# A planned single-core kernel: copies of y and of the outputs out of PSUM move from ScalarE to VectorE from token block 7 on, with a new order of all steps

## The chip, the cores and the metric

The kernel runs on one core of a Trainium2 chip. A core has five engines that run side by side, each with its own queue, in order: TensorE (matmuls; PE in the profile, its weight loads PEld), VectorE (DVE), ScalarE (ACT), GpSimd (POOL) and SyncE (SP, which here only issues DMAs). Matmul results land in PSUM, which GpSimd does not touch in this kernel; everything else is in SBUF. Engines wait for each other by semaphores. The metric is device time in microseconds of one launch; before the change the median of 13 runs is 299.23 us (295.42 to 300.69).

## What is computed

The reference is a gated linear recurrence followed by a gated feed-forward layer:

```python
q, k, v, a_re, a_im                     # (4, 8, 768, 48), fp32
mag = sqrt(a_re**2 + a_im**2)
scale = minimum(mag, 0.999) / (mag + 1e-6)
for t in range(768):                    # a = (a_re + i a_im) * scale
    S_re, S_im = ar*S_re - ai*S_im + k_t v_t^T, ar*S_im + ai*S_re
    y[:, :, t] = q_t @ S_re
x = y laid out as (3072 tokens, 384)
out = (sigmoid(x @ w_gate) * (x @ w_val)) @ w_out      # 384 -> 1536 -> 384
```

Inputs and output are fp32; the kernel's matmul operands are fp16 apart from the two prefix sums.

## The kernel before

The 3072 tokens are cut into 24 blocks of 128 (4 batches of 6 blocks), and these into ten groups of 1, 2, 2, 2, 3, 3, 3, 3, 3, 2 blocks (SIZES). A block m is (batch b, place c in the batch).

The recurrence is done in chunks. For each group ScalarE squares a (L597), GpSimd adds and clips (L614, L622), ScalarE takes logarithms and a reciprocal by exp (L629, L635, L640), GpSimd multiplies the ratio (L650) and ScalarE takes its arctangent (L714). For each block TensorE forms prefix sums of the log magnitude (`cl`, L656) and of the phase (`ct`, L734); ScalarE makes the decays e^(+-x/2) (`ee`, L662, L664), which GpSimd multiplies into q and k (L708); VectorE rounds the phase to whole turns (`r16`, L762), TensorE subtracts the turns (`nid`, L769), ScalarE makes sine and cosine (`cs`, L786 to L789), and VectorE multiplies them into k and q (`ks`, `qs`, L797). The k and q of a block are transposed by TensorE and copied by VectorE (`tp`, `qkT`, L838, L847) up to block 12, and by DMA (`xk`, `xq`, L820) from block 13 on (CROSS = 13). TensorE forms scores (`sc`, L859), VectorE masks them (`mst`, L868), and TensorE forms y (`y`, L933, L935) and the state update (`kv`, L904). VectorE carries the state (`u`, `P`, L885, L914) and GpSimd casts it to fp16 (`x16`, L895).

The phase runs on from block to block. In batch 0 GpSimd adds up a running sum (`run`, L750) which TensorE sums in (L737). In the other batches ScalarE copies the last row of a block's phase (`cr`, L777), a DMA from GpSimd's queue adds it to the first row of the next block's (`hop`, L726), and that block's `ct` waits for it.

Then y is copied out of PSUM and scaled to fp16 (`y16`), transposed (`xp`, L952) and copied (`xt`, L958). For a group the layer is done in 12 slices of 128 of the inner width: two matmuls of three steps each (`pg`, `pv`, L972), tanh on ScalarE (L982; the sigmoid is (tanh(x/2)+1)/2), the product on VectorE (`p`, L988), and the output matmul (`po`, L1007) for each block, in three parts. The output is copied out of PSUM with a factor 0.5 (`ot`) and stored from SP (`st`, L1025). ScalarE's functions lie in three table sets, loaded in turn (L1035). PSUM holds four buffers for the layer (`moe`) and four for the rest (`gen`).

Both copies out of PSUM go through one helper; the engine is chosen by the block's number:

```python
def scaled(m, dst, src, f):
    if m >= EASE:
        nc.vector.tensor_scalar(out=dst, in0=src, scalar1=f, scalar2=1.0,
                                op0=ALU.mult, op1=ALU.mult)
    else:
        nc.scalar.activation(out=dst, in_=src, func=FT.Copy, scale=f)
```

On ScalarE it is L517 in the profile, on VectorE L514. With EASE = 13, 13 blocks are on each side of y (13 and 11) and of the output (13, and 11 blocks with 12 copies, since the last block's output goes in two halves).

No loop nest sets the order. Every step is entered into a plan under a key such as ("y16", 7), with the steps it must follow, and the table TIMES holds one number for each step. The steps are sorted by that number and issued so, which fixes the order in each engine's queue. A second table, WARM, holds runs of matmuls on a zero tile (L1042) that are sorted in between, and the table loads stand in TIMES as well. The numbers are sort keys: no instruction waits for a time.

Of the kernel before, what the change touches and what calls it, by code (L numbers as in the profile page):

```python
# [27 lines left out]
EASE = 13  # L28
# [9 lines left out]
        12.8, 25.15, 38.52],  # L38
    "wo": [
        43.82, 55.48, 63.41],  # L40
# [3 lines left out]
        4.3, 7.5, 16.28, 25.26, 34.34, 41.35, 49.21, 65.37, 71.79,  # L44
        77.54, 86.69, 96.07, 100.42, 113.48, 117.83, 124.09, 136.17,
        143.42, 150.02, 165.27, 171.53, 176.33, 193.74, 203.66],
# [3 lines left out]
        7.5, 22.16, 40.13, 54.96, 83.64, 106.1, 133.38, 157.24, 181.89,  # L50
        208.31],
    "add": [
        8.05, 23.66, 26.43, 42.11, 45.62, 62.44, 66.74, 86.01, 87.1,
        88.59, 108.24, 110.3, 112.3, 135.68, 136.76, 138.25, 159.57,
        163.06, 164.66, 184.03, 191.35, 192.43, 212.12, 214.58],
    "min": [
        8.65, 25.92, 27.52, 45.1, 47.16, 65.26, 68.58, 88.08, 89.56,
        90.07, 113.78, 111.78, 114.29, 137.74, 139.23, 139.74, 161.99,
        164.15, 165.74, 185.12, 194.27, 194.79, 213.2, 218.63],
    "lna": [  # L60
        9.44, 29.36, 44.52, 66.4, 89.75, 117.39, 140.72, 169.31, 197.35,
        226.36],
    "lnm": [
        9.06, 28.66, 47.78, 69.2, 90.76, 118.4, 141.74, 170.32, 196.34,
        225.29],
    "inv": [
        9.99, 30.22, 45.39, 69.9, 91.78, 119.8, 142.75, 171.34, 198.54,
        227.23],
    "r": [
        10.53, 31.22, 32.2, 47.67, 49.15, 73.67, 72.7, 93.39, 95.85,  # L70
        94.36, 121.16, 123.11, 122.14, 145.09, 147.04, 146.06, 175.94,
        172.97, 173.95, 200.7, 199.73, 201.68, 229.64, 228.16],
    "cl": [
        9.61, 31.66, 30.85, 49.36, 48.72, 70.9, 72.96, 93.55, 92.05,
        92.91, 121.32, 120.68, 119.59, 145.23, 144.59, 143.3, 171.51,
        172.64, 173.28, 199.46, 200.1, 198.17, 226.53, 227.18],
    "ee": [
        10.46, 32.51, 31.7, 50.33, 49.57, 72.4, 74.46, 94.69, 93.17,
        93.93, 122.71, 121.57, 120.82, 146.2, 145.44, 144.15, 172.73,
        173.87, 174.63, 200.31, 201.45, 199.56, 227.93, 228.69],  # L80
    "scr": [
        11.39, 33.44, 33.89, 54.46, 54.01, 75.83, 75.38, 95.62, 94.1,
        94.86, 123.64, 122.63, 123.08, 148.22, 149.57, 148.67, 173.78,
        177.23, 182.25, 205.91, 203.21, 206.36, 230.06, 229.61],
    "rbe": [
        38.56, 37.66, 61.44, 79.79, 81.14, 97.77, 127.33, 129.58,
        154.94, 181.35, 192.84, 211.88, 232.21],
    "lq": [
        4.75, 17.18, 26.28, 42.25, 52.66, 60.09, 66.27, 78.44, 85.34,
        91.49, 101.77, 109.76, 115.28, 121.28, 128.23, 134.82, 141.12,  # L90
        146.87, 155.84, 163.26, 178.58, 186.8, 204.56, 218.56],
    "v16": [
        13.57, 28.03, 44.59, 52.66, 61.93, 74.65, 99.08, 96.83, 95.34,
        102.52, 113.27, 116.23, 124.09, 132.36, 152.69, 141.12, 153.2,
        160.54, 174.92, 204.14, 186.8, 220.57, 218.12, 238.22],
    "ke": [
        14.37, 36.57, 39.29, 57.23, 65.77, 81.51, 82.48, 97.34, 101.54,
        103.03, 129.64, 130.62, 124.6, 151.71, 153.71, 150.74, 177.89,
        176.92, 179.64, 210.11, 207.19, 209.14, 235.21, 234.24],
    "qe": [  # L100
        14.84, 33.44, 37.55, 54.51, 60.09, 79.56, 80.53, 99.59, 105.12,
        100.57, 127.69, 126.71, 128.66, 156.72, 148.01, 148.99, 188.08,
        180.62, 181.59, 208.16, 206.21, 203.16, 233.26, 246.07],
    "atan": [
        12.51, 34.73, 52.92, 77.43, 97.01, 124.76, 148.62, 177.43,
        204.25, 231.11],
    "ct": [
        13.06, 35.93, 37.21, 55.86, 58.12, 78.56, 82.31, 101.44, 107.1,
        112.62, 129.04, 134.69, 133.28, 153.06, 158.84, 164.42, 182.81,
        190.4, 187.16, 208.6, 214.6, 220.52, 235.08, 240.75],  # L110
    "run": [
        24.64, 35.59, 40.27, 56.25, 64.28],
    "r16": [
        13.91, 37.42, 38.7, 57.35, 60.04, 80.48, 83.17, 102.36, 107.96,
        113.48, 129.89, 136.01, 134.3, 153.91, 159.69, 165.27, 183.66,
        191.81, 188.01, 209.45, 215.74, 221.38, 235.93, 241.6],
    "nid": [
        14.51, 38.49, 41.59, 57.95, 60.65, 81.17, 83.77, 102.97, 108.61,
        114.08, 130.54, 136.61, 135.33, 154.52, 160.29, 166, 184.63,
        192.42, 188.94, 210.43, 216.43, 221.98, 236.53, 242.57],  # L120
    "cs": [
        14.88, 38.87, 41.96, 59.6, 61.13, 82.1, 86.54, 103.99, 109.63,
        114.83, 131.84, 137.89, 135.7, 155.27, 161.8, 166.37, 185.6,
        192.79, 190.44, 211.18, 217.71, 222.35, 237.94, 242.95],
    "ks": [
        16.32, 41.24, 50.13, 61.06, 67.72, 84.14, 90.58, 106.09, 115.37,
        116.74, 133.44, 142.49, 141.63, 157.7, 166.25, 169.05, 189.05,
        196.16, 193.41, 213.71, 219.7, 224.34, 239.37, 244.69],
    "qs": [
        17.33, 43.08, 51.13, 63.41, 70.62, 85.15, 92.01, 107.1, 117.61,  # L130
        118.47, 134.81, 144.22, 143.36, 158.7, 168.18, 170.48, 190.48,
        198.24, 195.3, 216.21, 222.31, 225.66, 242.53, 247.35],
    "tp": [
        18.77, 18.33, 44.55, 45.91, 52.58, 52.14, 69.37, 64.63, 75.24,
        74.79, 87.62, 86.15, 94.52, 95.61, 108.77, 110.07, 120.23,
        118.95, 124.08, 123.64, 135.82, 137.74, 147.41, 148.98, 146.48,
        147.85],
    "qkT": [
        19.58, 18.98, 45.2, 47.76, 54.65, 53.86, 70.02, 66.27, 76.04,
        75.45, 89.03, 88.43, 95.17, 96.26, 109.42, 110.73, 121.11,  # L140
        120.51, 124.89, 124.29, 137.27, 138.39, 148.06, 149.63, 147.13,
        148.66],
    "sc": [
        20.32, 19.77, 48.01, 48.5, 55.39, 54.59, 74.25, 70.46, 77.81,
        76.6, 92.69, 89.17, 96.22, 97.82, 112.01, 111.47, 122.18,
        121.96, 126.54, 125.12, 141.29, 139.13, 149.91, 152.09, 150.67,
        151.38, 166.65, 165.78, 175.03, 174.32, 178.93, 179.63, 201.88,
        195.35, 204.91, 205.62, 202.58, 203.29, 222.63, 223.99, 228.7,
        229.41, 231.19, 230.12, 248.89, 248.18, 252.58, 251.88],
    "mst": [  # L150
        20.8, 20.2, 48.44, 49.04, 56.31, 55.72, 74.68, 72.05, 79.24,
        77.74, 93.12, 89.96, 99.18, 99.77, 112.49, 111.9, 123.25,
        122.39, 126.97, 125.95, 145.09, 139.56, 151.63, 155.91, 154.84,
        152.23, 171.81, 167.12, 175.81, 174.75, 181.13, 180.07, 202.31,
        199.57, 206.28, 206.88, 203.01, 203.72, 223.17, 227, 229.14,
        230.2, 231.86, 230.8, 249.92, 248.86, 253.86, 253.26],
    "kv": [
        17.33, 44.99, 53.26, 76.4, 78.36, 100.51, 108.07, 116.59,
        124.52, 134.44, 148.29, 163.73, 169.3, 175.55, 191.53, 195.15,
        215.73, 224.21, 230.99, 241.88],  # L160
    "P": [
        18.19, 47.3, 55.25, 77.28, 81.71, 103.75, 108.76, 119.34,
        125.49, 136.47, 150.7, 164.52, 171.34, 176.41, 194.27, 199.11,
        221.84, 225.2, 233.19, 249.46],
    "y": [
        21.54, 50, 57.32, 76, 80.33, 97.09, 100.71, 115.22, 124.72,
        128.16, 145.87, 157.26, 156.56, 173.92, 181.04, 181.92, 204,
        207.72, 207.02, 227.82, 231.9, 233.48, 250.99, 260.91],
    "y16": [
        23.49, 51.09, 57.93, 77.05, 86.16, 98.67, 101.21, 119.42,  # L170
        127.99, 128.91, 146.95, 159.59, 159.97, 175.35, 181.73, 182.53,
        204.89, 210.38, 208.68, 228.62, 234.12, 234.58, 252.01, 261.56],
    "xp": [
        24.04, 54.12, 59.4, 79.84, 87.46, 99.97, 102.4, 122.5, 130.01,
        131.08, 155.86, 163.03, 160.94, 176.24, 185.33, 183.94, 206.32,
        211.12, 209.73, 230.34, 236.7, 235.72, 256.69, 262.49],
    "xt": [
        24.42, 56.91, 59.78, 80.22, 87.83, 100.37, 103.48, 122.99,
        132.4, 131.46, 160.15, 163.79, 163.53, 178.15, 186, 184.88,
        207.95, 217.8, 217.54, 232.46, 243.4, 245.56, 257.07, 263.17],  # L180
    "pg": [
        24.82, 25.58, 26.66, 30.24, 32.3, 34.9, 35.76, 41.42, 45.74,
        47.84, 53.09, 53.96, 60.18, 61.38, 62.45, 64.31, 69.81, 75.68,
        77.48, 80.01, 81.42, 82.96, 84.47, 86.6, 88.72, 94.2, 98.04,
        99.11, 100.18, 102.08, 103.15, 104.22, 105.29, 106.37, 108.28,
# [890 lines left out]
```

## Time and profile before

| | |
|---|---|
| median of 13 runs | 299.23 us (295.42 to 300.69) |
| the profiled execution, its time | 297.35 us |
| its span in the profile | 295.6 us |
| PE busy | 265.5 us (90%), of it 36.6 us warm-up matmuls (505) |
| DVE busy | 206.8 us (70%), 392 instructions |
| ACT busy | 208.3 us (70%), 362 instructions |
| POOL busy | 159.4 us (54%), 196 instructions |
| DMA | 38.54 MB, 130 GB/s over the span |

The busy time of an engine says how full its queue is, not who sets the end. For that the profile follows the chain of waits back from the last instruction: at each step to what released it. "Issue" there is time in which the engine waited for nothing that the profile shows. A busy PE includes the modelled ends of its matmuls, so its share is somewhat high. A granted clock of 1.00 is TensorE at full speed.

### The profile page before, as it was taken

What the parts mean: (1) busy time and instruction counts of PE and PEld (TensorE: products, weight loads), DVE (VectorE), ACT (ScalarE), POOL (GpSimd) and SP (SyncE); (2) the same over time, 40 slices, a digit from 0 to 9 for tenths busy, and PEclk for the clock granted to TensorE, in tenths of its full rate; (3) what the DMA queues carried; (4) which work ended last, traced back from release to release, by engine and by line L of the source; (5) the groups of instructions that cost most, each with busy time, mean ns of one, the idle gap of its engine ahead of it and who ended that gap; (6) DMA issues with size and microseconds to landing.
All of it is one profiled execution on the core that took longest, in us unless ns stands there. A gap on an engine that the chain in (4) does not pass through costs nothing.

```text
span 295.6 us, 6976 instructions
## 1 busy us (share of the span) xinstructions
PE 265.5 (90%) x2639; PEld 188.7 (64%) x2639; DVE 206.8 (70%) x392; ACT 208.3 (70%) x362; POOL 159.4 (54%) x196
## 2 busy tenths in 40 slices
PE   8798899789989869978998998979889999999996
PEld 8597789567766746656565555545545666666774
DVE  2246067778885698859877897697859986974542
ACT  2383977669799786979978799769955985422320
POOL 3017497694767868687585849843875172200000
PEclk9989999999999999999999999999999999999999
DMA  8997979998892945996694899749827822610103
GB/s 124 191 186 131 182 86 196 194 118 174 164 208 44 189 98 114 178 188 136 137 164 83 164 183 205 123 73 204 178 31 145 150 57 54 127 45 0 60 23 108
DMA packets 176033, 38.54 MB, mean 130 GB/s; under 512 B 168424, under 2 KB 176000, under 8 KB 176000
## 3 DMA queue, kind: packets, MB, share of 16 engines
q1 hardware_dynamic: 171536, 34.53, 61.0%
q0 software_dynamic: 4464, 3.56, 8.8%
q8 instruction: 21, 0.34, 0.5%
q14 instruction: 12, 0.10, 0.1%
HBM read 31.07 MB, written 4.76 MB: 121 GB/s over the span
## 4 chain that ended last, share of the span: by engine, by line
PE 40%; ACT 25%; DVE 16%; issue 8%; DMA 8%; SPq 2%; ACTq 0%; DVEq 0%
PE o L1007 9%; PE g L972 7%; PE v L972 7%; ACT L1035 5%; PE warm L1042 4%; PE ct L734 4%; ACT g L982 3%; DVE p L988 3%; DMA a<-cr 3%; DVE qkT L847 2%; DVE mst L868 2%; PE cl L656 2%; DVE kst L797 2%; DMA a<-in_a_im_dram 2%; DVE qst L797 2%
## 5 line engine op out<-in xcount | busy, mean ns | idle before, releaser
L982 ACT ACTIVATE g<-g 128x384 f16<-128x384 f32 (+2 forms) x120 | 48.7, 424 | 47.0 <-PE g L972 44.3
L988 DVE SCALAR_TENSOR_TENSOR p<-g,v 128x384 f16<-128x384 f16 (+2 forms) x120 | 55.3, 469 | 30.3 <-ACT g L982 23.3
L972 PE MATMUL g<-xt,wg 128*128 128x384 f16 (+2 forms) x360 | 66.5, 294 | 5.1 <-ACT g L982 5.0
L972 PE MATMUL v<-xt,wv 128*128 128x384 f16 (+2 forms) x360 | 66.5, 294 | 2.5 <-ACT g L982 1.3
L1007 PE MATMUL o<-wo,p 128*128 128x384 f16 (+1 forms) x300 | 55.8, 320 | 0.0
L972 PEld LDWEIGHTS <-wg 128*128 128x128 f16 x360 | 32.8, 97 | 24.3 <-issue 13.0
L708 POOL TENSOR_TENSOR qk<-qk,ee 128x384 f32<-128x384 f32 x46 | 46.9, 1108 | 0.5
L972 PEld LDWEIGHTS <-wv 128*128 128x128 f16 x360 | 32.0, 97 | 16.8 <-issue 6.1
L1007 PEld LDWEIGHTS <-p 128*128 128x128 f16 x300 | 28.3, 98 | 16.5 <-issue 1.4
L1035 ACT ACT_TABLE_LOAD x29 | 37.2, 1283 | 0.5
L1042 PE MATMUL warm<-zero 128*128 128x128 f16 x505 | 36.6, 234 | 1.0 <-DVE zero L491 1.0
L868 DVE TENSOR_TENSOR mst<-sc,msk_t 128x512 f16<-128x512 f32 x48 | 32.0, 685 | 5.4 <-PE sc L859 5.3
L1042 PEld LDWEIGHTS <-zero 128*128 128x128 f16 x505 | 33.6, 106 | 3.1 <-issue 1.3
L614 POOL TENSOR_TENSOR lm<-sq 128x384 f32<-128x384 f32 x23 | 26.2, 1157 | 15.2 <-ACT sq L597 14.6
L895 POOL CAST x<-u 128x384 f16<-128x384 f32 x20 | 15.1, 755 | 33.4 <-DVE u L885 27.0
L650 POOL TENSOR_TENSOR a<-a 128x384 f32<-128x384 f32 x23 | 23.0, 1020 | 17.5 <-ACT a L640 17.4
L797 DVE TENSOR_TENSOR kst<-qk,cs 128x768 f16<-128x768 f32 x24 | 27.8, 1163 | 4.5 <-ACT cs L789 3.2
L734 PE MATMUL ct<-a,wt_t 128*128 128x384 f32 x48 | 20.3, 506 | 5.5 <-DMA a<-cr 2.4
L797 DVE TENSOR_TENSOR qst<-qk,cs 128x768 f16<-128x768 f32 x24 | 24.7, 1036 | 0.0
L656 PE MATMUL cl<-lm,wl_t 128*128 128x384 f32 x48 | 19.8, 520 | 3.6 <-ACT lm L635 3.5
L699 POOL TENSOR_SCALAR v<-v 128x384 f16<-128x384 f32 x24 | 14.1, 589 | 14.8 <-DMA v<-in_v_dram 13.0
L847 DVE COPY qkT<-tp 128x1024 f16<-128x1024 f16 x26 | 17.3, 686 | 5.9 <-PE tp L839 5.8
(64 smaller groups left out, 430.7 us busy)
## 6 DMA issues: line engine op xcount, KB each, us to landing
a<-in_a_re_dram SPq DMA_DIRECT2D x24, 192.0 KB
a<-in_a_im_dram SPq DMA_DIRECT2D x24, 192.0 KB
qk<-in_k_dram SPq DMA_DIRECT2D x24, 192.0 KB
qk<-in_q_dram SPq DMA_DIRECT2D x24, 192.0 KB
v<-in_v_dram SPq DMA_DIRECT2D x24, 192.0 KB
out_dram<-ot SPq DMA_DIRECT2D x23, 192.0 KB
wg<-in_moe_w_gate_dram POOLq DMA_DIRECT2D x3, 384.0 KB, 5.2
wv<-in_moe_w_val_dram POOLq DMA_DIRECT2D x3, 384.0 KB, 5.2
```

The costliest lines, as they stand in the source:

```text
L614: eng(g).tensor_tensor(out=T[LM][:, s], in0=T[SQ][:, 0, s], in1=T[SQ][:, 1, s], op=ALU.add)
L656: nc.tensor.matmul(T[CL][:, :HD], wl_t, T[LM][:, s], start=True, stop=True)
L708: eng(g).tensor_tensor(out=qk, in0=qk, in1=T[EE][:, i], op=ALU.mult)
L734: nc.tensor.matmul(ct, wt_t, T[A][:, 1, s], start=True, stop=False, skip_group_check=True)
L797: nc.vector.tensor_tensor(out=T[SL][i].rearrange("p h (r x) -> p h r x", r=2)[:, :, :, 0:D], in0=heads(T[QK][:, i]).unsqueeze(2) .broadcas ...
L868: nc.vector.tensor_tensor(out=T[MS], in0=T[SC], in1=msk_t.unsqueeze(1).broadcast_to([L, 4, L]), op=ALU.mult)
L972: nc.tensor.matmul(T[ACC][:, :nt], w[:, j, fb * 128:fb * 128 + 128], T[XT][:, j, :nt], start=(j == 0), stop=(j == 2))
L982: nc.scalar.activation(out=T[G16][:, :nt], in_=T[PG][:, :nt], func=FT.Tanh, scale=0.5)
L988: nc.vector.scalar_tensor_tensor(out=T[PT][:, fb, :nt], in0=T[G16][:, :nt], scalar=1.0, op0=ALU.add, in1=T[PV][:, :nt], op1=ALU.mult)
L1007: nc.tensor.matmul(T[PO][:, :wd], T[PT][:, fb, s * L:(s + 1) * L], wo16[:, fb, c0:c0 + wd], start=(fb == 0), stop=(fb == NFB - 1))
L1035: nc.scalar.preload_act_table_set(SETS[key[1]])
L1042: nc.tensor.matmul(acc[:, :L], zero, zero, start=True, stop=True)
```

## The change

EASE goes from 13 to 7: `y16` and `ot` of blocks 7 to 12 are done by VectorE in place of ScalarE. TIMES and WARM are replaced as a whole; the helper, the steps and what they wait for are as before. WARM goes from 42 runs with 505 matmuls to 37 runs with 446. The file is five lines shorter, so a line of the kernel after is five lower than here below the tables.

```diff
 CROSS = 13
-EASE = 13
+EASE = 7
 ROLL = 1
...
     "la": [
-        4.3, 7.5, 16.28, 25.26, 34.34, 41.35, 49.21, 65.37, 71.79,
-        77.54, 86.69, 96.07, 100.42, 113.48, 117.83, 124.09, 136.17,
-        143.42, 150.02, 165.27, 171.53, 176.33, 193.74, 203.66],
+        4.3, 7.5, 16.28, 25.26, 32.56, 42.06, 46.41, 58.27, 68.11,
+        73.86, 80.61, 87.41, 95.22, 111.21, 115.66, 123.17, 133.57,
+        140.4, 146.15, 162.66, 169.36, 174.16, 190.64, 199.59],
...
     "run": [
-        24.64, 35.59, 40.27, 56.25, 64.28],
+        24.64, 35.13, 38.44, 54.92, 57.18],
...
     "table": [
-        11.485, 13.695, 27.93, 33.535, 36.32, 43.24, 51.925, 58.765,
-        65.62, 75.48, 81.32, 88.965, 95.715, 100.43, 116.11, 123.735,
...
+        11.645, 13.865, 27.43, 32.235, 34.88, 44.84, 52.205, 54.995,
+        64.12, 69.775, 73.265, 84.345, 93.375, 97.175, 113.845, 121.465,
...
```

What the order does around the steps that the prediction speaks of, engine by engine:

- ScalarE before: tanh, tanh, y16(3), arctangent of blocks 5 and 6, tanh, tanh, table load, sines of block 5, tanh, square of blocks 7 to 9. After: tanh, tanh, the arctangent, table load, tanh, tanh, sines of block 5, y16(3), tanh, tanh, y16(4), the square.
- GpSimd before: run(3), k of block 3, q of block 4, v16(4), an addition of block 5, a load of w_out, run(4). After: run(3), a load of w_out, x16(2), run(4), k of block 3, v16(3), the addition, a load of w_out.
- SP before: a of block 7, k, q and v of block 6, a of block 8, the decays of blocks 6 and 5, a of block 9. After: a of block 7, k, q and v of block 5, a of block 8, k, q and v of block 6, a of block 9, the decay of block 5.
- VectorE after, around the moved copies: y16(7) between `ks` and `qs` of block 8; y16(8) ahead of the `xt` of block 8; y16(9) ahead of two `p`; y16(10) between two `qkT`; y16(11) and y16(12) ahead of `ks` of block 13; ot(8) and ot(7) ahead of a `mst` of block 14; ot(9) ahead of `qs` of block 16; ot(10) and ot(12) ahead of y16(16); ot(11) after `ks` of block 20.

## The prediction

> **What bounds the kernel now.** I read the chain of waits by engine first, then the busy time of the engines in stretches, then the pieces of the chain that belong to the copies that move, and last the groups of instructions for durations. The sum is made against the profiled execution: span 295.6 us, time 297.35 us. The median of the 13 runs, 299.23 us, lies 1.88 us above that, and a difference in us is carried over to it.
>
> ```profile
> PE 40%; ACT 25%; DVE 16%; issue 8%; DMA 8%; SPq 2%; ACTq 0%; DVEq 0%
> ```
>
> No engine owns the chain. TensorE has the largest part, yet 60% of the end is set by something that TensorE waits for, and ScalarE is the first of those.
>
> ```profile
> 60.00:112.00 52.00, 45.11 (x478) 34.09 (x477) 41.55 (x75) 43.58 (x79) 37.09 (x45) 1.00 0.78 139
> 112.00:170.00 58.00, 51.92 (x499) 34.95 (x497) 47.28 (x87) 49.95 (x89) 42.66 (x52) 1.00 0.78 149
> 170.00:230.00 60.00, 54.01 (x445) 32.96 (x443) 47.98 (x85) 49.26 (x84) 38.07 (x44) 1.00 0.78 144
> ```
>
> Columns: stretch, its length, then busy us of PE, its weight loads, DVE, ACT and POOL, the granted clock, DMA share, GB/s. In each stretch TensorE idles some 6 to 7 us (6.9, 6.1, 6.0), with ACT busy 84, 86 and 82% and DVE 80, 82 and 80%. ACT and DVE are within 5 points of each other. After 230 us PE is busy to the end (31.04 of 32, 30.62 of 34), so what is won or lost before that is carried to the end.
>
> **Part 1, twelve copies from ACT to DVE.** The threshold moves for blocks 7 to 12: six copies of y and six of the output. In the built programs ACT goes from 26 such copies to 14 and DVE from 23 to 35, and that is all that the threshold does. No DMA is added.
>
> ```profile
> L517 ACT ACTIVATE ot<-o 128x384 f32<-128x384 f32 x13 | 6.4, 493 | 0.2 <-PE o L1007 0.2
> L517 ACT ACTIVATE y<-y 128x384 f16<-128x384 f32 x13 | 6.4, 501 | 5.1 <-PE y L935 5.1
> L514 DVE TENSOR_SCALAR y<-y 128x384 f16<-128x384 f32 x11 | 6.0, 550 | 0.2 <-PE y L935 0.2
> L514 DVE TENSOR_SCALAR ot<-o 128x384 f32<-128x384 f32 x10 | 5.6, 557 | 8.9 <-PE o L1007 8.8
> ```
>
> Removed from ACT: 6 x 0.501 + 6 x 0.493 = 5.96 us. Added to DVE: 6 x 0.550 + 6 x 0.557 = 6.64 us. The six y copies fall in 112 to 170 us (starts 119.5 to 162.9), the six output copies in 170 to 230 us (175.8 to 226.6). ACT becomes 46.9 of 58 (81%) and 46.3 of 60 (77%); DVE 50.6 of 58 (87%) and 51.3 of 60 (86%). So the fuller engine is no emptier than before; the two change places.
>
> What the ACT part is worth is read from the chain of waits: of the twelve, five stand on it.
>
> ```profile
> 119.64 0.38 ACT y L517
> 128.53 0.24 ACT y L517
> 129.57 0.39 ACT y L517
> 175.78 0.49 ACT ot L517
> 176.91 0.51 ACT ot L517
> ```
>
> Together 2.01 us. (The first delays the reciprocal that ACT runs next, for blocks 10 to 12; the last two stand before and between the exponentials of blocks 16 to 18.) A check by shares: ACT is 25% of the chain, 73.9 us of its 208.3 busy, 35%; 35% of 5.96 is 2.1. **Gain 2.0 us.** The other seven are hidden by ACT's waits for TensorE, and removing them is worth nothing.
>
> What DVE pays cannot be read off, since the copies are not there yet. Between 0 (all in DVE's 10.7 and 12.0 us of idle time in the two stretches) and 6.64 us (all on the path) I take DVE's own share: 16% of 295.6 is 47.3 us on the chain of 206.8 busy, 23%, so **1.5 us lost**. What waits behind them: in the new DVE order the copy of y for block 7 stands between the two products of the rotation (k and q) of block 8, those for blocks 11 and 12 stand together ahead of the k product of block 13, and the output copies of blocks 8 and 7 stand ahead of the mask of block 14. Each of those feeds TensorE. Part 1: -0.5 us, ends -2.0 and +4.6.
>
> Here a rule speaks against the change. The Trainium skill, "SBUF — State Buffer" (section "SBUF: two separate sides"), says that DVE and GpSimd share one port pair under an exclusive lock, which a DVE operation with two SBUF inputs needs while GpSimd reads SBUF; the loser waits for the whole instruction. The row of this case:
>
> ```profile
> L797 DVE TENSOR_TENSOR kst<-qk,cs 128x768 f16<-128x768 f32 x24 | 27.8, 1163 | 4.5 <-ACT cs L789 3.2 <-POOL qk L708 1.1 <-POOL lm L614 0.2
> ```
>
> Its shortest is 945 ns and its longest 2373 ns, so 24 of them hold 5.1 us of stretching (27.8 - 24 x 0.945), as the rule would have it. The copies that move have one input, in PSUM, and range over 547 to 558 ns: they do not stretch. By the rule read broadly (DVE work beside a busy GpSimd is dearer than its row) each copy would cost up to one stretch of a neighbour, at worst 1.4 us more (2.37 - 0.95) where it pushes a product into a GpSimd instruction; by the row it costs 0.55. I take the row, and keep one stretch for the slower case.
>
> **Part 2, warm-up matmuls.** 505 become 446. One takes 0.056 us (a chain piece of 38 took 2.12). Up to the first phase matmul of block 3 (57 us) there are 45 fewer, 2.5 us; later 14 fewer, 0.8 us.
>
> ```profile
> 39.70 1.96 PE warm L1042 x35
> 43.44 2.12 PE warm L1042 x38
> 47.55 1.34 PE warm L1042 x24
> 60.76 0.50 PE warm L1042 x9
> ```
>
> The first three are on the chain, but from 40 to 60 us the DMA share is 1.06 and 1.03: taken away, the wait for data takes their place, worth 0 (end -2.5). The fourth stands where TensorE has work to do next: **-0.5 us** (ends -0.8 and 0). A rule against it: the Trainium skill, "TensorE: Matmul & The Clock Gate" (Part 1, "The HAM clock gate"), says the clock is halved after about 3.4 us without enough work and comes back after about 3.4 us of it. This trace grants 1.00 from 20 us to 290 us, 0.83 in 10 to 20 us alone, and the longest wait that the view of waits gives a matmul after that is 1.7 us (rounding before L769). By the rule a stretch left bare would cost an estimated 1.7 us each (3.4 us of work at half speed); by the row none. I take none and keep 1.7 for the high end.
>
> **Part 3, the new order.** Every engine's queue is re-sorted, also before block 7. What I can follow in the rows:
> - GpSimd: the running phase sum of block 4 (L750) moves ahead of two decay products and the value copy (L708, L699). In the trace SP sat 3.5 us waiting for it before it could load a for block 7, and 1.6 us for a decay of block 5 before block 9; both loads can go earlier. But the square that needs them (ACT, 81.18 us) has no idle time before it: worth 0 there. For SP's later loads, which stand behind these in one queue, it is cover against a late transfer.
> - ACT: the table load (L1035, 1.28 us) ahead of the sines of block 5 moves ahead of two tanh. In the trace ACT waits for TensorE at the second of them:
>
> ```profile
> 77.96 0.38 ACT L982 ACTIVATE g<-g 128x256 f16<-128x256 f32 x1 [1.90 <-PE g L972]
> 78.36 1.28 ACT L1035 ACT_TABLE_LOAD   x1
> 79.66 0.49 ACT L786 ACTIVATE cs<-ct 128x384 f32<-128x384 f32 x1
> 81.18 2.13 ACT L597 ACTIVATE sq<-a 128x2304 f32<-128x2304 f32 x1
> ```
>
> (Columns: start, us, then idle time before it and its releaser.) From 79.66 to 97 us ACT is busy without a break and on the chain. In the new order the load fits into the 1.90 us of waiting, so 1.28 us leave that run; the y copy of block 3, done before at 74.56 us in easy time, moves into it: 0.50 us. Net -0.78.
> - The serial chain of phase sum, rounding, carry and hop by DMA (L734, L762, L777, L726) keeps its steps: DMA a<-cr is 2.6% of the chain, 7.7 us, and table loads are 4.7%, 13.9 us. No order removes them.
>
> I take **-0.8 us**. TensorE's idle time from 60 to 230 us is 19.0 us, of which an order of hundreds of steps can give back more, or add to it; as ends I take a fifth of it, -4 and +3.
>
> **Sum.** -0.5 - 0.5 - 0.8 = -1.8 us: 297.35 becomes 295.55 for such an execution, and 299.23 becomes **297.4 us**, 0.6% less. Its own range is 296 to 298.7 us.
>
> **Rivals.** (a) **DVE becomes the bound**, slower. It goes to 87 and 86% busy, and the p products (L988), which free the g and v banks, queue behind the copies. For it: the stretching falls on DVE alone. Against: in 112 to 230 us p waited 9.5 us for ACT's tanh, so DVE was often the earlier of the two. It decides once half of the added 6.64 us is on the path, since 2.0 + 0.5 + 0.8 = 3.3 us are to be paid back. With all of it there, +3.3 us: 302.6 us. (b) **The hop paces blocks 6 to 22.** In 170 to 230 us DMA a<-cr is 12.9% of the chain; a copy that leaves ACT only lengthens the wait for the hop, and the lead of part 3 is used up at the first one. Then the 0.5 us of part 2 is left: 298.7 us, no change. (c) **The order gives back more**: TensorE's idle time shrinks by the fifth named above and DVE hides the copies, -2.0 - 0.5 - 4 at most; I price it at -4.5: 294.7 us. (d) The change not doing what it says: excluded by the count of copies in the built programs.
>
> **How the numbers follow.** Forecast 0.45, (a) 0.33, (b) 0.07, (c) 0.15. Within 0.5% (1.5 us, about what a measurement of this kernel can tell from nothing) means 297.7 to 300.7 us. A third of the forecast's own range lies in it, and (b): same 0.15 + 0.07 = 0.22; faster 0.30 + 0.15 = 0.45; slower 0.33. The range runs from (c) with 1 us more (293.7) to (a) in full (302.6).
>
> **What would show it.** Right: ACT copies 14 and DVE copies 35; ACT 46 to 47 us and DVE 50 to 52 us in these two stretches; the sines of block 5 follow their tanh with no table load between; the waits of p for ACT shorter; clock 1.00 after 20 us. Wrong: PE idle over 6 us in 112 to 170 us with p or the rotation products named as releasers (a); DMA a<-cr with a larger share of the chain and the same end (b); PE clock below 1 between 40 and 60 us; or the start up to 60 us longer by more than 1 us, which none of my parts has.

## The result, and the profile after

The kernel after takes **295.31 us** (median of 11 runs, 293.82 to 298.13) beside 299.24 us for the kernel before: ratio 0.9893 [0.9866, 0.9919], which is 3.2 us or 1.1% less [2.4 to 4.0 us]; the medians lie 3.9 us apart. Times of runs are told below by their ratio, which compares runs on the same chip. The profiled execution took 294.35 us. Three lines of the page of the kernel after: the span, the engines' busy time, the chain of waits by engine.

```profile
span 292.5 us, 6898 instructions
PE 260.3 (89%) x2580; PEld 182.5 (62%) x2580; DVE 210.2 (72%) x404; ACT 203.8 (70%) x350; POOL 161.1 (55%) x196
PE 29%; ACT 19%; DVE 11%; issue 11%; DMA 10%; POOL 9%; SPq 9%; ACTq 0%; DVEq 0%; POOLq 0%
```

TensorE's part of the chain falls from 40 to 29%; ScalarE's and VectorE's fall too, although VectorE took on the copies. The busy time also shows what a copy costs in a full queue: the rows said 0.49 and 0.50 us, but ScalarE is only 4.5 us less busy for twelve of them, 0.37 each. The recorded durations of neighbours overlap: where ScalarE doesn't wait, the next instruction mostly starts 0.37 to 0.39 us after a copy.

The same stretches as before, and the start, by windows (PE, its weight loads, DVE, ACT, POOL, clock, DMA share, GB/s):

```profile
40.00:60.00 20.00, 17.46 (x222) 13.37 (x221) 15.33 (x31) 17.79 (x31) 16.34 (x19) 1.00 1.01 159
60.00:112.00 52.00, 45.25 (x463) 32.46 (x461) 40.65 (x76) 42.21 (x76) 40.22 (x48) 1.00 0.79 147
112.00:170.00 58.00, 52.17 (x498) 34.88 (x496) 50.37 (x93) 49.63 (x84) 41.25 (x48) 1.00 0.79 151
170.00:230.00 60.00, 54.51 (x455) 33.49 (x454) 52.45 (x93) 47.99 (x79) 36.94 (x42) 1.00 0.82 152
```

VectorE has 50.4 and 52.5 us where 47.3 and 48.0 were. TensorE idles 5.8 and 5.5 us there, 0.7 us less in all than before: the two stretches with the moved copies hold little of the 3.2 us. In 40 to 60 us TensorE is busy 0.7 us less although it gets further: 74 warm-up matmuls fewer run there (60 in place of 134).

Where the lead arises is read by laying equal work side by side. The phase sum of block 3 (`ct`) begins at 54.4 us in place of 56.8, the logarithm for the decays of blocks 5 and 6 (L635, L630 after) at 64.1 in place of 68.7, the square of blocks 7 to 9 at 77.2 in place of 81.2, `ct` of block 7 at 97.0 in place of 100.1, and at the end 3.1 us are left. So in these two executions **the whole lead is there by 65 us**, nearly 50 us ahead of the first moved copy, which runs at 112.1 us. What follows has only to keep it.

The waits of VectorE say what became of the part that was meant for the copies. From 170 to 230 us, in the kernel after (us in all, times, longest):

```profile
DVE p L983 <- ACT g L977: 2.8, 3, 2.0
DVE ot L509 <- PE o L1002: 1.5, 1, 1.5
DVE r L757 <- PE ct L729: 1.1, 2, 0.6
DVE kst L792 <- ACT cs L784: 0.9, 1, 0.9
```

The first line was 5.8 us before; with the stretch before it, p waits 3.6 us for the tanh in place of 9.5.

### The profile page after: what moved, and what is told of

The parts are those of the page before. It is cut to its first block, busy times and chain, and to the rows that moved or that the text cites. A ratio compares the mean times of both kernels' runs of the same rounds, so it can differ in the third digit from the quotient of the medians.

```text
span 292.5 us, 6898 instructions
## 1 busy us (share of the span) xinstructions
PE 260.3 (89%) x2580; PEld 182.5 (62%) x2580; DVE 210.2 (72%) x404; ACT 203.8 (70%) x350; POOL 161.1 (55%) x196
## 4 chain that ended last, share of the span: by engine, by line
PE 29%; ACT 19%; DVE 11%; issue 11%; DMA 10%; POOL 9%; SPq 9%; ACTq 0%; DVEq 0%; POOLq 0%
PE o L1002 8%; PE g L967 7%; PE v L967 6%; SPq L549 6%; DMA v<-in_v_dram 4%; DVE p L983 3%; PE ct L729 3%; ACT L1030 3%; ACT g L977 3%; POOL qk L703 3%; DMA a<-in_a_im_dram 2%; POOL a L645 2%; SPq L673 2%; ACT ee L657 2%; DMA a<-cr 2%
## 5 line engine op out<-in xcount | busy, mean ns | idle before, releaser
L977 ACT ACTIVATE g<-g 128x384 f16<-128x384 f32 (+2 forms) x120 | 48.1, 423 | 46.9 <-PE g L967 44.7
L1002 PE MATMUL o<-wo,p 128*128 128x384 f16 (+1 forms) x300 | 55.0, 320 | 0.3 <-DVE p L983 0.3
L703 POOL TENSOR_TENSOR qk<-qk,ee 128x384 f32<-128x384 f32 x46 | 47.6, 1077 | 1.1
L645 POOL TENSOR_TENSOR a<-a 128x384 f32<-128x384 f32 x23 | 24.0, 1063 | 27.6 <-ACT a L635 12.6
L609 POOL TENSOR_TENSOR lm<-sq 128x384 f32<-128x384 f32 x23 | 24.8, 1109 | 14.6 <-ACT sq L592 14.3
L792 DVE TENSOR_TENSOR kst<-qk,cs 128x768 f16<-128x768 f32 x24 | 26.8, 1121 | 6.6 <-ACT cs L784 4.8
L1037 PE MATMUL warm<-zero 128*128 128x128 f16 x446 | 30.3, 227 | 1.3 <-DVE zero L486 1.0
L1037 PEld LDWEIGHTS <-zero 128*128 128x128 f16 x446 | 27.9, 102 | 3.8 <-issue 2.2
L890 POOL CAST x<-u 128x384 f16<-128x384 f32 x20 | 12.3, 616 | 24.4 <-DVE u L880 24.1
L757 DVE TENSOR_SCALAR r<-ct 128x384 f16<-128x384 f32 x24 | 13.3, 554 | 12.4 <-PE ct L729 8.4
```

The costliest lines, as they stand in the source:

```text
L609: eng(g).tensor_tensor(out=T[LM][:, s], in0=T[SQ][:, 0, s], in1=T[SQ][:, 1, s], op=ALU.add)
L645: eng(g).tensor_tensor(out=T[A][:, 1, s], in0=T[A][:, 1, s], in1=T[A][:, 0, s], op=ALU.mult)
L703: eng(g).tensor_tensor(out=qk, in0=qk, in1=T[EE][:, i], op=ALU.mult)
L792: nc.vector.tensor_tensor(out=T[SL][i].rearrange("p h (r x) -> p h r x", r=2)[:, :, :, 0:D], in0=heads(T[QK][:, i]).unsqueeze(2) .broadcas ...
L977: nc.scalar.activation(out=T[G16][:, :nt], in_=T[PG][:, :nt], func=FT.Tanh, scale=0.5)
L1002: nc.tensor.matmul(T[PO][:, :wd], T[PT][:, fb, s * L:(s + 1) * L], wo16[:, fb, c0:c0 + wd], start=(fb == 0), stop=(fb == NFB - 1))
```

## What happened at the start

VectorE's timeline of the kernel before (start, us, then the idle time before it):

```profile
41.20 1.71 DVE L797 TENSOR_TENSOR kst<-qk,cs 128x768 f16<-128x768 f32 x1 [1.06 <-POOL qk L708]
43.02 1.55 DVE L797 TENSOR_TENSOR qst<-qk,cs 128x768 f16<-128x768 f32 x1
46.84 0.89 DVE L885 TENSOR_TENSOR u<-P,arr 128x384 f32<-128x384 f32 x1
62.02 2.37 DVE L797 TENSOR_TENSOR kst<-qk,cs 128x768 f16<-128x768 f32 x1 [0.21 <-POOL lm L614]
64.98 1.67 DVE L797 TENSOR_TENSOR qst<-qk,cs 128x768 f16<-128x768 f32 x1
```

Undisturbed these take 0.945 (kst, qst) and 0.56 us (u). The five are stretched by 0.76, 0.61, 0.33, 1.43 and 0.72 us, 3.8 us together. GpSimd's timeline of the kernel before shows what it did beside the fourth:

```profile
61.72 0.81 POOL L545 DMA_DIRECT2D wo<-in_moe_w_out_dram  x1
62.56 1.01 POOL L750 TENSOR_TENSOR run<-run,a 128x384 f32<-128x384 f32 x1
63.65 1.10 POOL L622 TENSOR_SCALAR lm<-lm 128x384 f32<-128x384 f32 x1
```

The product holds on through the issue of a load and the running sum, and ends at 64.39. In the kernel after that running sum runs at 56.70 us, and of the same five only one is stretched, by 0.3 us:

```profile
58.81 0.36 DVE L953 COPY xt<-xp 128x384 f16<-128x384 f16 x1 [0.40 <-PE xp L947]
59.90 1.25 DVE L792 TENSOR_TENSOR kst<-qk,cs 128x768 f16<-128x768 f32 x1 [0.74 <-ACT cs L784]
61.07 0.41 DVE L983 SCALAR_TENSOR_TENSOR p<-g,v 128x256 f16<-128x256 f16 x1
```

The new order does not end such collisions, it puts fewer of them elsewhere. In the same stretch an `arr` that took 0.16 us takes 0.96, and a kst at 65.6 us takes 1.16; with them the start loses 1.3 us to collisions in place of 3.8. Over the whole kernel kst and qst take 50.9 us in place of 52.5. The runs below test how much of the result this start is, and what the copies add.

## The experiments

**Copies and order apart.** The two halves of the change alone, then the two copies alone in the new order. Each ratio is to the kernel before.

```diff
 # old_order_ease7: kernel before
-EASE = 13
+EASE = 7
 # new_order_ease13: kernel after
-EASE = 7
+EASE = 13
 # new_order_y_dve: kernel after, only y moves
-        if m >= EASE:
+        if m >= (EASE if f != 0.5 else 13):
 # new_order_ot_dve: kernel after, only the output moves
-        if m >= EASE:
+        if m >= (EASE if f == 0.5 else 13):
```

> The old order and old warm-ups, with the twelve copies on VectorE. Theory S (the traces: TensorE is already 3 us ahead at 65 us, before any moved copy): the copies are worth nothing by themselves, 0 to +1 us against before. The prediction's part 1: -0.5 us, with -2.0 if VectorE hides all of them. Rival (VectorE becomes the bound): +2 us or more, since this order made no room for them.

> The new order and new warm-ups, with the twelve copies back on ScalarE. Theory S: the whole gain stays, ratio 0.987 to 0.992 (-2.5 to -4 us). If the copies bring 2 us of the 3.2, some 1.2 us are left, ratio 0.996. If the new order leans on ScalarE being relieved, no gain or a loss.

> The kernel after once more, as the base that the next three are held against on the same chip: ratio to before 0.987 to 0.992.

> The new order; of the twelve copies only the six of y are on VectorE, the six of the outputs are back on ScalarE. Theory C (in the new order a y copy on ScalarE stands behind the sine of a block two further on, and TensorE waits for it; an output copy delays ScalarE's exponentials): part of the 3.2 us is kept, ratio 0.992 to 0.997. If the y copies alone matter: 0.989.

> The new order; only the six output copies are on VectorE, the six of y back on ScalarE. Theory C: ratio 0.993 to 0.998, the other part is lost, with TensorE waiting 1.3 us for the y copy of block 7 at the transposition that follows it (L947). If the output copies alone matter: 0.989.

| | copies from block 13 | copies from block 7 |
|---|---|---|
| old order | 1 | 1.0001 [0.9967, 1.0035] |
| new order | 1.0009 [0.9973, 1.0045] | 0.9893 [0.9866, 0.9919]; again 0.9898 [0.9857, 0.9939] |

Neither half does anything that can be measured, and both together give 3.2 us. Theory S, by which the new order keeps its gain without the copies, is refuted by this. In the old order twelve copies on the other engine are worth nothing; in the new order they are worth 1.1%, 3.3 us. Of these the y copies alone keep little that is certain (0.9981 [0.9950, 1.0012]), the output copies alone about half (0.9951 [0.9917, 0.9985]).

For the copies of y the reason is in the view of who waited for the line of ScalarE's copies. In new_order_ease13 (us in all, times):

```profile
PEld L947: 3.9, 4
PE xp L947: 2.5, 3
```

and in after_again, where seven y copies are left on ScalarE:

```profile
PEld L947: 0.6, 2
PE xp L947: 0.2, 1
```

(PEld and PE can be two sides of one wait, so they are not added.) In the kernel before, the same view gives 0.4 and 0.2: there no transpose waits for a copy to speak of. What a copy waits behind in the new order is seen in the timeline of ScalarE in new_order_ease13:

```profile
114.80 0.57 ACT L772 ACTIVATE cr<-ct,lst_t 32x384 f32<-32x384 f32 x1 [3.49 <-PE ct L764]
115.39 0.49 ACT L781 ACTIVATE cs<-ct 128x384 f32<-128x384 f32 x1
115.78 0.48 ACT L782 ACTIVATE cs<-ct 128x384 f32<-128x384 f32 x1
116.29 0.61 ACT L784 ACTIVATE cs<-cs,pio 128x384 f32<-128x384 f32 x1
116.81 0.47 ACT L512 ACTIVATE y<-y 128x384 f16<-128x384 f32 x1
```

TensorE had this y ready at 114.2 us. The copy stands behind a carry that waits 3.49 us (until 114.80) and behind the three steps of a sine and cosine, and starts 2.6 us late; the transpose that needs it starts at 117.33 after 1.27 us of idle TensorE. In the kernel after, VectorE copies the same y 1.2 us after it is ready. The new order has a slot for these copies in VectorE's queue and none in ScalarE's.

The output copies are seen in the same view of new_order_y_dve, where only they are on ScalarE:

```profile
PE v L967: 0.8, 1
PEld L947: 0.6, 2
PE g L967: 0.4, 1
PE xp L947: 0.2, 1
```

There TensorE waits 1.2 us for output copies before it can start a `pv` and a `pg`; in the kernel after 0.4 us of such waits are left, for VectorE's copies. new_order_ease13 has both the waits for y and those for the outputs. So each half of the copies has waits of its own in the new order when it stays on ScalarE. How these waits add up to 3.3 us was not followed to the end.

**The start alone.** The sort keys ahead of table load 8, counted from 0 (64 us in the new order, 66 in the old), come from one kernel, the later ones from the other, with 500 added so that they sort behind; the warm-ups go with their half.

```diff
 # new_start_old_rest: keys of "la" as an example; 453 warm-up matmuls
-        4.3, 7.5, 16.28, 25.26, 34.34, 41.35, 49.21, 65.37, 71.79,
+        4.3, 7.5, 16.28, 25.26, 32.56, 42.06, 46.41, 58.27, 571.79,
 # new_start_old_rest_ease7: the same, and
-EASE = 13
+EASE = 7
```

> New order up to the eighth table load (some 65 us), then what is left in the old order, copies as before on ScalarE. Theory S: -2.5 to -3.5 us, ratio 0.988 to 0.992. Rival (the later order makes the gain, or the lead is lost at the first hop): 0 to -1 us.

> New order up to the eighth table load, the rest in the old order, and the twelve copies on VectorE. If the copies keep what the start wins also in the old later order: ratio 0.989 to 0.992. If they do so only in an order made for them: 0.993 to 0.996, as with the copies on ScalarE (0.9946).

> Old order up to the eighth table load (some 66 us), then what is left in the new order, the twelve copies on VectorE. Theory S: 0 to -1 us. Rival (the later order and the copies make the gain): -2 to -3 us.

New start with the old rest: 0.9946 [0.9913, 0.9980], 1.6 us less. With the copies on VectorE as well: 0.9930 [0.9891, 0.9969], not told apart from it. The old start with the new rest and the copies: 0.9986 [0.9951, 1.0020], nothing that can be measured. So the start gives about half of the result by itself, less than the 2.5 us that theory S asked for at least. In all profiles with the old start, old_run_early apart, the five stretches above are there, to within 40 ns; in those with the new start only the 0.3 us of one product, as in the kernel after.

That half is not the order alone. In its profile new_start_old_rest begins the square of blocks 19 to 21 at 184.4 us and old_order_ease7, with the old start on the same chip, at 188.1; at the end 0.8 us are left. In between the hop takes 5.1 us to land (3.7 in old_order_ease7), TensorE waits 1.8 us for it, and then runs at half clock for 3.41 us (PE busy, clock, DMA share, GB/s):

```profile
184.13:187.54 3.41, 1.45 (x21) 1.00 0.70 91
187.54:190.95 3.41, 3.41 (x12) 0.50 0.90 173
```

The profiles of the other two mixed kernels have such a stretch too, from 105.43 and 109.90 us; those of the kernels before and after have none between 20 and 290 us. How much of the missing half is the clock, and how much the order, is not separated.

**Single pieces of the start and of part 3.**

```diff
 # old_few_warm: kernel before without the runs of WARM from 55 us on
-    (55.615, 0, 3),
-    (59.570, 0, 9),
...
-    (96.058, 1, 3),
 # old_run_early: kernel before, "run" of block 4
-        24.64, 35.59, 40.27, 56.25, 64.28],
+        24.64, 35.59, 40.27, 56.25, 56.26],
 # old_table_early: kernel before, table load 10, ahead of two tanh
-81.32
+77.435
```

> The old order without its last warm-up matmuls (from the run at 55.6 in the list on, 59 of 505). Prediction part 2: -0.5 us. Rival: nothing, since other waits take their place. The clock stays 1.00 after 20 us[...].

(46 matmuls are left out, 459 of 505 remain; the 59 of this text is a miscount.)

> The old order with one GpSimd step moved: the running phase sum of block 4 goes right behind that of block 3. Theory L (the 2.37 us of the k product of block 3 at 62 us are 1.4 us of waiting for GpSimd's load of w_out and this sum): the product takes 1.4 to 2.0 us, SP's 3.5 us wait goes, the time falls by 0.5 to 1 us. Prediction part 3: the loads go earlier but are worth 0 by themselves.

> The old order with one step of ScalarE moved: the table load ahead of the sines of block 5 goes ahead of two tanh. Prediction part 3: -1.28 us in ScalarE's run from 80 us on, and most of it kept to the end. Rival: the tanh wait for TensorE anyway and the hop paces what follows: 0.

old_few_warm: 0.9932 [0.9902, 0.9962], 2.0 us less [1.1 to 2.9]. Their own time is 46 x 0.056 = 2.6 us: by the ratio a warm-up in a stretch where TensorE has work costs most of what it takes. The one profile of this kernel does not show where: its phase sum of block 15 begins at 166.5 us, 0.9 us ahead of the kernel before, and 0.45 us of that are there at 36 us, ahead of the first warm-up that is left out. The granted clock stayed at 1.00 in every window from 20 to 262 us. The collisions remain in that kernel (kst 2.37 us at 61.6), so this gain is not theirs.

old_table_early: 0.9973 [0.9937, 1.0009], -0.8 us with zero inside the interval. It fits the -0.78 of part 3 and does not prove it.

old_run_early went the other way: 1.0112 [1.0056, 1.0169], **slower** by 3.4 us. It did what was meant on VectorE, where kst is back to 0.96 us and qst to 0.95. But on GpSimd a load of w_out stands behind the sum that moved ahead, and is issued at 63.71 in place of 61.72 us; it took 6.07 us to land in place of 4.93. TensorE's waits from 60 to 75 us in old_run_early, where the kernel before has none:

```profile
PE o L1041 <- DMA wo<-in_moe_w_out_dram: 3.1, 1, 3.1
```

The phase sum of block 5 then begins 3.2 us later than in the kernel before (79.14 for 75.89 us), while that of block 4 was level (59.04 for 59.12), so this wait is of the size of the loss. It is seen in one execution only, of 307.39 us; the other five took 300.6 to 304.9 us. In the kernel after the load moved with the running sum, and is issued at 60.28.

**One collision taken out of the kernel after.** The longest product in its trace, that of block 16, runs beside three additions of GpSimd in a row. GpSimd, then VectorE, then TensorE in the kernel after:

```profile
186.91 3.15 POOL L609 TENSOR_TENSOR lm<-sq 128x384 f32<-128x384 f32 x3
187.78 3.11 DVE L792 TENSOR_TENSOR kst<-qk,cs 128x768 f16<-128x768 f32 x1 [0.91 <-ACT cs L784]
191.42 0.32 PE L764 MATMUL ct<-r,nid_t 128*128 128x384 f16 x1 [1.71 <-DVE r L757]
```

The rounding r stands behind the product, and TensorE waits 1.71 us for it. Here the product goes behind r, an xt and two p:

```diff
 # after_ks16_later: kernel after; "ks" of block 16, and "xk" of block 16
-184.34
+187.5
-185.34
+187.6
```

> The kernel after, with one step moved on VectorE: the k product of block 16, which in its trace takes 3.11 us beside three GpSimd additions, goes behind the rounding of block 18, a copy of x and two p products. Theory L (such a product waits for GpSimd, and what stands behind it on VectorE waits along): it takes some 1 us, TensorE's wait for the rounding (1.7 us) goes, and the time falls by 1 to 2 us against the kernel after, ratio to before 0.983 to 0.987. If the hop or the loads pace this stretch anyway: no change against the kernel after.

VectorE's timeline in after_ks16_later:

```profile
190.07 0.56 DVE L791 TENSOR_SCALAR r<-ct 128x384 f16<-128x384 f32 x1 [1.74 <-PE ct L763]
190.54 0.35 DVE L987 COPY xt<-xp 128x384 f16<-128x384 f16 x1
190.81 1.02 DVE L1017 SCALAR_TENSOR_TENSOR p<-g,v 128x384 f16<-128x384 f16 x2
191.75 1.18 DVE L826 TENSOR_TENSOR kst<-qk,cs 128x768 f16<-128x768 f32 x1
```

The product takes 1.18 us, and TensorE's wait is gone. Time: **294.04 us**, 0.9849 [0.9799, 0.9899] of the kernel before, 1.4 us below after_again (295.41) on the same chip. It has the lowest median of the versions run here and came as expected. Its interval and that of after_again overlap, so the 1.4 us are not clear of the noise; that the wait goes is seen.

## The prediction, point by point

The direction was right and the time lay in the range. The sum of -1.8 us was too small by 1.4 us against the ratio's -3.2 (297.4 is 2.1 us above the median); the result lies between it and rival (c). That the sum came so near was in part luck: the order alone, priced at -1.3 us with its warm-ups, gave +0.3, the copies alone, priced at -0.5, gave 0.0, and no term of the sum stands for what comes only when both are there.

- **Part 1, -0.5 us.** Alone it measured 0.0 us, with -1.0 to +1.1 as its interval, so the sum of gain and loss for the old order was right within what can be told. The step that failed is the adding of the parts: parts 1 to 3 were priced each against the old order and summed. In the new order the same twelve copies are worth 3.3 us; the copy of block 7, if it stays on ScalarE, stands there behind a queue of 2.6 us, where on the old chain it held its own 0.4 us.
- **VectorE's load** came as worked out: 50.4 and 52.5 us for 50.6 and 51.3. That 1.5 us of it would be on the path did not show: TensorE idles no more than before in either stretch. ScalarE's 46 to 47 us did not come (49.6 and 48.0): other work of its queue moved into these stretches.
- **The rule of the port pair.** The copies did not stretch (545 to 559 ns in the kernel after, the two half-size ones at the end apart), as taken. But the rule decided more than the part it was weighed in. It was asked what it adds to twelve copies, and not which stretches the new order takes away or makes. Five were gone from the start; that of block 16 grew from 1.0 to 2.2 us, and the kernel with this product moved is 1.4 us faster, not clear of the noise. The "one stretch, 1.4 us" kept for the slower case was of this size.
- **Part 2, -0.5 us** for 14 later warm-ups. 46 of them measured 2.0 us, which in proportion is 0.6 us for 14: it fits. In the profiles before and after no clock was lost between 20 and 290 us, as taken. But the reason given, that the longest wait of 1.7 us is below 3.4, does not hold: in two of the mixed kernels the clock was halved beside waits of 1.4 and 1.8 us (see the last section). The 45 early ones at "worth 0" were not tried alone; they went with the start.
- **Part 3, -0.8 us.** The order alone measured +0.3 us [-0.8, +1.3] with the warm-ups of part 2 in it, so the -1.3 of both did not come without the copies. The term mis-sized here is the stretch before 57 us, put at nothing: early warm-ups 0, earlier loads 0. The start measured -1.6 us [-2.6, -0.6]. Nor was the running sum free to move: alone, ahead of the load of w_out, it costs 3.4 us.
- **Rivals.** (a), VectorE as the bound, fell twice: the copies alone cost nothing, and together they gain. (b) fell with the gain. (c), 294.7 us, is about as near in size as the sum, but by another way than its fifth of TensorE's idle time after 60 us: from 60 to 230 us that idle time fell by 0.9 us, and in the traces the lead is older.

Of what was to show it: 14 and 35 copies, the shorter waits of p, the sines of block 5 after their tanh with no table load between, and the clock were right. A start over 1 us *longer* was named as a sign of error; that it could be as much shorter was not thought of.

Not settled: how the start's 1.6 us divide between early warm-ups, the five stretches and the rest of its order. The 2.0 us of old_few_warm and the 1.6 us overlap, since the new start has fewer warm-ups too. The early warm-ups are the rival to be tried first: from 36 to 66 us they hold 25.9% of the chain of waits (7.8 us) in the kernel before, and 0.7 us in the kernel after.

## What to carry over

An engine assignment and an order written for it are one change: run both halves alone before either is judged, and price a copy by what stands ahead of it in its queue, and not only by its own duration. When an order is made anew, list the products of VectorE that run longer than their shortest instance, and see which of them feeds TensorE; moving one step past a busy GpSimd removed a wait of 1.7 us here. And when a step moves, look at the loads that stand behind it in its queue: one sum moved alone cost 3.4 us.

## What the runs showed of the hardware

A product of VectorE waited not for one GpSimd instruction but for three in a row (3.11 us beside 3.15 us of additions): it didn't get in between them. These stretches are not chance; the one of 3.11 us is 3.12 us in the second profile of the same kernel.

What differs from one execution to the next is the landing of small DMAs. The two profiled executions of the kernel after (294.35 and 297.12 us) agree within 0.3 us up to 179 us, and within 0.04 us from 160 us on. Then the hop a<-cr, issued at 179.33 and 179.37, lands in 3.3 us in one and 5.1 us in the other. Waits of TensorE from 160 to 188 us in after_again:

```profile
PE ct L729 <- DMA a<-cr: 2.2, 1, 2.2
```

In the first execution that wait is 0.5 us. The product at 187.78 then starts at 189.64, so 1.9 of the 2.8 us between the two is this one landing. A pair of single profiles can therefore show a difference of 2 us that isn't the kernel's; the ratios above are over 6 to 48 runs.

The granted clock is the other thing that differs. In these profiles it is halved for 3.41 us at a time or a multiple of that, on a grid of 3.41 us that runs through the whole execution (in new_start_old_rest from 13.46 and from 187.54 us, 51 steps apart). Cut on this grid from 20 to 262 us, the 14 profiles of this case hold six stretches of 3.41 us in which TensorE was busy, by the profile, for less than 45% (10 to 44.5%), and each is followed by one at half clock; after none of the others (45.0% and more) is the clock halved. Single waits of 1.4 to 3.1 us lie in these six.

The gain of the change is not a matter of the clock. Of the executions on one chip whose mean clock is at least 0.997, the five of after_again have a median of 295.4 us and the five of the kernel before one of 298.9 us.
